# Identity passes ahead of late weights, and a split of the third group's spectra, in a sparse attention plus spectral mixing kernel

## The chip, the cores and the metric

The kernel runs on one core of a Trainium2 chip. The time is the device time of one execution in microseconds (us). Five runs of the kernel before gave a median of 431.25 us (430.57 to 432.88). The profile is of one of these runs, which took 432.25 us.

The engines are TensorE (PE in the profile; PEld is its weight load), VectorE (DVE), ScalarE (ACT), GpSimd (POOL) and SyncE (SP). Transfers run on 16 DMA engines. The weights come in through the queue that POOL issues to, the results go out through SP's.

## The reference

For 8 batches, 8 heads, 576 tokens and a head size of 64, a sparse attention (half of the heads local, half with a stride of 32) gives `x` of 8 x 576 x 512. Then, in the shortest form:

```
X  = rfft(x, axis=1)[:, :64]                 # 64 modes
Yr = Xr @ w_r[m] - Xi @ w_i[m]               # one 512 x 512 pair of weights per mode
Yi = Xr @ w_i[m] + Xi @ w_r[m]
y  = irfft(Y, n=576)
u  = x + y
out = u + relu(u @ w_ch)                     # float32, 8 x 576 x 512
```

The weights `w_r` and `w_i` are 64 x 512 x 512 float32 each, 134 MB in all, and each is used once.

## The kernel before, in words

**The modes.** A mode has two halves (256 rows of the weights each), so there are 128 half-modes, walked in the list `ORDER`. `w_fetch` (line 155) fetches two neighbouring modes of a half into one tile `wt` with 128 partitions: the real part goes to partitions 0 to 63, the imaginary part to 64 to 127, and the transfer turns float32 into float16. Normally that is one transfer of 512 KB for the real and one for the imaginary part. For the last two tiles (modes 60 and 61, modes 62 and 63 of the second list) each mode has a transfer of its own, 256 KB each, in the order: real of the first mode, real of the second, imaginary of the first, imaginary of the second (line 180). Tiles live in a pool of five buffers; after every second mode `mode` (line 544) calls `w_fetch`, whose transfer waits until TensorE has done with the buffer that it takes. POOL's queue is in order, and each of its transfers also waits for the one eight before it.

`mode(slot, m)` makes 16 matmuls (128 x 16, line 555) into a PSUM tile `y`; every eight modes the tile is moved to `Y0` or added into `YT` (lines 581 and 583). The last two modes, 62 and 63, have a small addition of their own.

**The last stage.** The last 24 half-modes are in the list `rest` (line 978), counted by `i` from 0. Between them stand the pieces of the list `late` (line 896), handed out by a share of their number (line 983): from `i` = 1 on, `i` + 1 pieces have been done after mode number `i`, and none after `i` = 0. The pieces are, in this order:

- `spec_pair(2, bq)` for the two halves of the batch (line 874). Spectra of group 2 (modes 32 to 47, already complete) are multiplied with `w_ch` into `zp` (4 matmuls, line 672) and turned into `yp` (4 matmuls, line 679). Both lie in one PSUM pair tile `u`. Then for each of four batches `spec_out` (line 685) copies 32 rows of `zp` to `zzs[b]` with ScalarE (line 687, in the profile line 241) and 32 rows of `yp` to `yys[b]` with VectorE (line 688). The scheduling layer orders two engines' reads of one PSUM tile one behind the other, as they are written.
- `renew(b, ts)` (line 881), 20 times: the kept product `v0` is put into a PSUM tile `v` by an identity matmul (line 889), the group's rows are added (line 696), ScalarE copies it back to `v0` (line 891, shown as 241); then the same rows for `u`, which VectorE adds to `xo` (line 894). It takes two token blocks at a time; four times (after the odd batches) it takes one, the last 64 tokens of two batches. `v` has one buffer, `u` has two.

After mode 61 (`i` = 21) `v_early(0)` and `u_early(0)` put the first output item's kept values into PSUM by identity matmuls (lines 921 and 930), and between modes 62 and 63 `u_early(1)` does so for the second.

**The tail.** When mode 63 is in, the spectra of the last group are made (lines 996 and 997), and for 20 output items in turn the last rows are added (line 941), ScalarE takes the relu (line 955), VectorE adds (line 963) and SyncE writes to memory (lines 971 and 974).

Of the kernel before, what the change touches and what calls it, by code (L numbers as in the profile page):

```python
# [15 lines left out]
B = 8  # L16
# [40 lines left out]
def kernel(  # L57
# [10 lines left out]
    nc = tc.nc  # L68
# [16 lines left out]
    def psum(kind, half=False, pair=False):  # L85
        if pair:
            return pss[kind].tile([128, 2, 512], FP, tag=kind, name=kind)
        if half:
            return pss[kind].tile([128, 1024], F16, tag=kind, name=kind)
        return pss[kind].tile([128, 512], FP, tag=kind, name=kind)  # L90
# [19 lines left out]
    idn = cs["cI"]  # L110
# [44 lines left out]
    def w_fetch(n=1):  # L155
        for _ in range(n):
            i = len(w_tiles)
            if i >= 2 * NM:
                return
            half, m = ORDER[i]  # L160
            if i // 2 in GUEST:
                wt = big.tile([128, 2, 4, DM], F16, tag=GUEST[i // 2], name="wt")
            else:
                wt = pw.tile([128, 2, 4, DM], F16, tag="w", name="wt")
            for ri, src in enumerate((moe_w_r, moe_w_i)):
                dst = wt[ds(64 * ri, 64)]
                rows = src[m : m + 2, ds(256 * half, 256), :].rearrange(
                    "m (p c) e -> p m (c e)", c=4
                )
                dst = dst.rearrange("p m c e -> p m (c e)")  # L170


                ones = range(2)
                if ri and not m:
                    ones = [1]
                elif i < 2 * NM - 4:
                    nc.gpsimd.dma_start(dst, rows)  # L177
                    continue
                for j in ones:
                    nc.gpsimd.dma_start(dst[:, j], rows[:, j])  # L180
            w_tiles.extend((wt[:, 0], wt[:, 1]))

    def w_ch_fetch():
# [56 lines left out]
    def act_copy(out, in_):  # L240
        nc.scalar.activation(out=out, in_=in_, func=ACTF.Copy)  # L241
# [302 lines left out]
    def mode(slot, m):  # L544
        half = 1 - slot
        mi, mg = m % 8, m // 8
        if mi == 0:
            ypt[slot] = psum("y")
        yp = ypt[slot]
        yv = yp.rearrange("p (m e x) -> p m e x", m=8, e=4)  # L550
        wt = w_tiles[ORDER.index((half, m))]
        pr = ds(0, 128 if m else 64)
        for e in range(4):
            for c in range(4):
                nc.tensor.matmul(  # L555
                    yv[:, mi, e, :],
                    wt[pr, XC[c], ds(128 * e, 128)],
                    Xh[half][pr, c, :, :, m],
                    start=(c == 0),
                    stop=(c == 3),  # L560
                )
        if m % 2 and (slot or m // 2 not in GUEST):
            w_fetch()
        ends = {7: 8}
        if slot and mg == 7:
            ends = {5: 6, 7: 2}
        if mi in ends:
            n = ends[mi]
            m0 = mi + 1 - n
            part = (  # L570
                slice(None),
                slice(None),
                mg // 2,
                slice(None),
                ds(8 * (mg % 2) + m0, n),
            )
            src = yp.rearrange("p (m e x) -> p e x m", m=8, e=4)[:, :, :, ds(m0, n)]
            if slot == 0:
                if m == 7:
                    spectra_tile("Y0")  # L580
                nc.scalar.activation(out=YS["Y0"][part], in_=src, func=ACTF.Copy)
            else:
                nc.vector.tensor_tensor(
                    out=YS["YT"][part], in0=src, in1=YS["Y0"][part], op=AluOp.add
                )
# [51 lines left out]
    v0s, xos = {}, {}  # L637
# [31 lines left out]
    def spec_z(g, bq, zp):  # L669
        for e in range(4):  # L670
            lhs = YS["YT"][:, e, g, ds(8 * bq, 8), :].rearrange("p x m -> p (x m)")
            nc.tensor.matmul(
                zp, lhs, w_chs["n"][:, e, :], start=(e == 0), stop=(e == 3)
            )

    def spec_y(g, bq, yp):
        for e in range(4):
            lhs = YS["YT"][:, e, g, ds(8 * bq, 8), :].rearrange("p x m -> p (x m)")
            nc.tensor.matmul(yp[:, ds(128 * e, 128)], lhs, idn, start=True, stop=True)

    def spec_mm(g, bq, yp, zp):
        spec_z(g, bq, zp)
        spec_y(g, bq, yp)

    def spec_out(g, b, yp, zp):
        src, dst = ds(32 * (b % 4), 32), ds(32 * g, 32)
        act_copy(zzs[b][dst], zp[src])
        nc.vector.tensor_copy(out=yys[b][dst], in_=yp[src])

    def rows_of(b, t, acc, spectra, fresh):  # L690
        if t < 4:
            todo = [(acc, out_cols(t), b)]
        else:
            todo = [(acc[ds(64 * j, 64)], ds(512, 64), b - 1 + j) for j in range(2)]
        for o, cols, bb in todo:
            nc.tensor.matmul(  # L696
                o, cA[0:96, cols], spectra[bb][0:96], start=fresh, stop=True
            )
# [75 lines left out]
    for b in range(B):  # L774
# [12 lines left out]
        n = 0  # L787
        nm = NMODES[b]
        for mi in range(nm):
            upto = -(-len(work) * (mi + 1) // nm)  # L790
            for w in work[n:upto]:
                w()
            n = upto
# [7 lines left out]
    xoh = [ptr.tile([128, DM], F16, name=f"xoh{i}") for i in range(4)]  # L801
    zzs = [ptr.tile([128, DM], F16, name=f"zz{i}") for i in range(B)]
    yys = [ptr.tile([128, DM], F16, name=f"yy{i}") for i in range(B)]
# [56 lines left out]
    n = 0  # L860
    for m in range(SPLIT0):
        mode(1, m)
        upto = -(-len(work) * (m + 1) // SPLIT0)
        for w in work[n:upto]:
            w()
        n = upto
# [4 lines left out]
    yctx = ctx.enter_context(ExitStack())  # L871
    pss["y"] = yctx.enter_context(tc.tile_pool(name="ps_y2", bufs=2, space=PSUM))

    def spec_pair(g, bq):
        up = psum("u", pair=True)
        zp, yp = up[:, 0], up[:, 1]
        spec_mm(g, bq, yp, zp)
        for b in range(4 * bq, 4 * bq + 4):
            spec_out(g, b, yp, zp)

    def renew(b, ts):
        n = len(ts)
        if n == 2:
            v0, xo = v0s[b][:, ts[0] : ts[0] + 2], xos[b][:, ts[0] : ts[0] + 2]
        else:
            v0, xo = v0h[b // 2].unsqueeze(1), xoh[b // 2].unsqueeze(1)
        vp, up = psum("v", pair=True), psum("u", pair=True)
        for j, t in enumerate(ts):
            nc.tensor.matmul(vp[:, j], idn, v0[:, j], start=True, stop=False)
            rows_of(b, t, vp[:, j], zzs, False)  # L890
        act_copy(v0, vp[:, 0:n])
        for j, t in enumerate(ts):
            rows_of(b, t, up[:, j], yys, True)
        nc.vector.tensor_tensor(out=xo, in0=up[:, 0:n], in1=xo, op=AluOp.add)  # L894

    late = [lambda bq=bq: spec_pair(2, bq) for bq in range(2)]
    for b in range(B):
        for t in (0, 2):
            late.append(lambda b=b, t=t: renew(b, (t, t + 1)))
# [3 lines left out]
    def units_of(item):  # L903
        P, t = item
        return [(2 * P + j, t) for j in range(2 if t < 4 else 1)]

    items = []
# [5 lines left out]
    vps, ups, rls, osbs = {}, {}, {}, {}  # L913

    def own(item, kept, half):
        P, t = item
        return [kept[b][:, t] for b, _ in units_of(item)] if t < 4 else [half[P]]
# [5 lines left out]
    def v_early(k, stop=False):  # L923
        vps[k] = psum(("v", "v2")[k % 2], pair=True)
        v_own(k, stop)

    def u_early(k):
        ups[k] = psum("u", pair=True)
        for j, r in enumerate(own(items[k], xos, xoh)):
            nc.tensor.matmul(ups[k][:, j], idn, r, start=True, stop=False)  # L930

    def new_rows(k, acc, spectra):
        P, t = items[k]
# [45 lines left out]
    n = 0  # L979
    NL = len(rest) - 2  # L980
    for i, (slot, m) in enumerate(rest):
        mode(slot, m)
        upto = min(len(late), -(-len(late) * i // (NL - 1)))
        for w in late[n:upto]:
            w()
        n = upto
        if i == NL - 1:
            v_early(0)
            u_early(0)
        elif i == NL:  # L990
            u_early(1)
    yctx.close()
    with tc.tile_pool(name="ps_s", bufs=1, space=PSUM) as pss["s"]:
        zp = pss["s"].tile([128, 512], FP, name="zp")
        yp = pss["s"].tile([128, 512], FP, name="yp")
# [15 lines left out]
    for k in range(2, LAST + 2):  # L1011
        if k <= LAST:
            v_early(k)
        if k == 4:
            held = vps[k][:, 1]
            spec_z(3, 1, held)
        if k == 5:
            held = vps[k][:, 1]
            spec_y(3, 1, held)
        if k > 2:  # L1020
            u_early(k - 1)
        if k <= LAST:
            new_rows(k, vps[k], zzs)
        if k > 2:
            new_rows(k - 1, ups[k - 1], yys)
        if k <= LAST:
            v_done(k)
        if k in (4, 5):
            act_copy((zzs, yys)[k - 4][1], held)
        if k > 2:  # L1030
            u_done(k - 1)
# [31 lines left out]
```

The softmax here doesn't subtract the row's maximum and nothing guards it: scores larger than these inputs give would overflow.

## Time and profile before

| what | value |
|---|---|
| median of 5 runs | 431.25 us |
| the profiled execution: time, span | 432.25 us, 430.5 us |
| busy: PE, DVE, ACT, POOL | 347.9, 238.9, 205.7, 107.4 us |
| moved by DMA | 91.78 MB, of which 81.28 MB on POOL's queue |
| weights: transfers of 512 KB | 62 and 60, 18 to 19 us from issue to landing |

The span is the time between the first and the last instruction. The part of the execution outside it is 1.75 us. "Busy" of TensorE is not TensorE at its peak: its matmuls overlap. The row PEclk tells the share of its full clock that TensorE was granted. The DMA row and its GB/s tell how full the 16 transfer engines were.

### The profile page before, as it was taken

The numbers are of one execution on the slowest core, as the hardware profiler recorded it, in microseconds if no ns is written. First come the engines' busy times: TensorE is split into PE (matmuls) and PEld (weight loads), VectorE is DVE, ScalarE is ACT, GpSimd is POOL, SyncE is SP. The second block draws the span as 40 slices with busy tenths as digits, with TensorE's granted clock in tenths as the row PEclk, the third lists the DMA queues.
The fourth block names the chain that finished last, engine by engine and source line by source line (L and its number), as shares of the span: only waits on it lengthen the run. The fifth ranks groups of instructions, "written<-read, shape, count | busy, mean of one in ns | idle before, by whom it ended". The sixth has DMA issues, their size and how long they took to land.

```text
span 430.5 us, 12303 instructions
## 1 busy us (share of the span) xinstructions
PE 347.9 (81%) x5431; PEld 240.9 (56%) x5431; DVE 238.9 (55%) x465; ACT 205.7 (48%) x361; POOL 107.4 (25%) x191
## 2 busy tenths in 40 slices
PE   2977888779989787987477698888898759987994
PEld 2866776658767575765345455565565525543331
DVE  3788778835425444443104246854784455554784
ACT  1687678644645454656132223522442354443773
POOL 8332332322423222221221222222222212310000
PEclk9999899966969998899756769988999968999997
DMA  8999999999999999999999999999999999992698
GB/s 150 209 211 213 212 214 212 211 210 212 214 212 214 214 213 214 214 214 211 212 213 214 213 214 214 215 212 213 213 214 215 213 214 214 213 208 51 238 359 282
DMA packets 30485, 91.78 MB, mean 213 GB/s; under 512 B 4001, under 2 KB 4769, under 8 KB 30433
## 3 DMA queue, kind: packets, MB, share of 16 engines
q0 software_dynamic: 24704, 81.28, 95.5%
q1 hardware_dynamic: 5216, 9.52, 6.2%
q8 instruction: 42, 0.69, 0.6%
q10 hardware_dynamic: 512, 0.21, 0.2%
q14 instruction: 11, 0.08, 0.0%
HBM read 162.83 MB, written 9.44 MB: 400 GB/s over the span
## 4 chain that ended last, share of the span: by engine, by line
DMA 51%; PE 27%; DVE 11%; ACT 5%; issue 3%; POOL 1%; DVEq 0%; ACTq 0%; POOLq 0%
DMA wt<-in_moe_w_i_dram 43%; DMA wt<-in_moe_w_r_dram 7%; PE y L555 4%; DVE xb L231 3%; DVE kz L273 3%; PE v L921 2%; PE tp L403 2%; PE y L522 2%; PE u L930 2%; PE sc L449 2%; PE sc L522 2%; ACT X L241 2%; PE v L941 1%; PE sc L465 1%; DMA ring<-in_v_dram 1%
## 5 line engine op out<-in xcount | busy, mean ns | idle before, releaser
L555 PE MATMUL y<-X,wt 128*128 128x16 f16 (+1 forms) x2048 | 82.7, 192 | 29.8 <-DMA wt<-in_moe_w_i_dram 28.5
L555 PEld LDWEIGHTS <-wt 128*128 128x128 f16 (+1 forms) x2048 | 72.7, 101 | 43.9 <-issue 35.9
L177 POOL DMA_DIRECT2D wt<-in_moe_w_r_dram x62 | 36.4, 588 | 168.3 <-PE y L555 97.9
L177 POOL DMA_DIRECT2D wt<-in_moe_w_i_dram x60 | 35.4, 591 | 49.6 <-DMA wt<-in_moe_w_i_dram 38.1
L653 PE MATMUL sc<-w_cp,xT 128*128 128x512 f16 (+1 forms) x160 | 46.7, 419 | 0.0
L662 ACT ACTIVATE v<-sc 128x512 f16<-128x512 f32 x32 | 19.1, 597 | 55.9 <-PE sc L653 55.8
L479 ACT ACTIVATE PL<-sc 128x480 f16<-128x480 f32 (+1 forms) x48 | 27.3, 579 | 34.4 <-PE sc L465 34.1
L663 DVE COPY xo<-tp 128x512 f16<-128x512 f16 x32 | 22.1, 691 | 32.2 <-PE tp L661 32.1
L231 DVE TENSOR_TENSOR xb<-av,rec 90x256 f16<-90x256 f32 (+2 forms) x80 | 36.0, 450 | 2.7
L230 DVE RECIPROCAL rec<-av 90x4 f32<-90x4 f32 (+2 forms) x80 | 14.6, 183 | 35.9 <-PE av L494 24.5
L410 DVE COPY qT<-tp 128x576 f16<-128x576 f16 x16 | 12.0, 758 | 35.5 <-PE tp L403 32.6
L894 DVE TENSOR_TENSOR xo<-u,xo 128x1024 f16<-128x1024 f32 x16 | 19.6, 1225 | 15.9 <-PE u L696 15.8
L241 ACT ACTIVATE v<-tp 128x640 f16<-128x640 f16 (+1 forms) x24 | 19.4, 808 | 17.7 <-PE tp L437 15.1
L403 PE MATMUL tp<-cI_s,ring 64*64 64x64 f16 x864 | 25.5, 205 | 2.5 <-issue 1.6
L368 ACT ACTIVATE PL<-sc 90x360 f16<-90x360 f32 (+1 forms) x48 | 22.7, 490 | 7.0 <-PE sc L361 6.4
L963 DVE TENSOR_TENSOR osb<-u,rl 128x1024 f32<-128x1024 f32 (+1 forms) x21 | 22.2, 1071 | 5.5 <-PE u L941 3.4
L241 ACT ACTIVATE v<-v 128x1024 f16<-128x1024 f32 x16 | 16.4, 1023 | 18.0 <-PE v L696 18.0
L403 PEld LDWEIGHTS <-ring 64*64 64x64 f16 x864 | 19.7, 118 | 7.7 <-issue 3.9
L449 PE MATMUL sc<-cMl_s,cI_s 128*128 128x480 f16 (+1 forms) x48 | 20.7, 430 | 3.3 <-ACT PL L479 1.6
L266 PE MATMUL tp<-cI_s,ring 72*128 72x72 f16 x256 | 15.4, 207 | 8.8 <-DMA ring<-in_v_dram 7.2
L955 ACT ACTIVATE rl<-v 128x1024 f32<-128x1024 f32 (+1 forms) x21 | 18.8, 901 | 6.6 <-PE u L941 4.1
L522 PEld LDWEIGHTS <-xb 108*128 108x128 f16 (+2 forms) x176 | 15.2, 106 | 12.0 <-DVE xb L231 7.4
(128 smaller groups left out, 695.8 us busy)
## 6 DMA issues: line engine op xcount, KB each, us to landing
wt<-in_moe_w_r_dram POOLq DMA_DIRECT2D x62, 512.0 KB, 18.2
wt<-in_moe_w_i_dram POOLq DMA_DIRECT2D x60, 512.0 KB, 19.4
out_dram<-osb SPq DMA_DIRECT2D x15, 512.0 KB, 3.2
ring<-in_v_dram POOLq DMA_DIRECT2D x8, 288.0 KB, 13.4
ring<-in_q_dram POOLq DMA_DIRECT2D x8, 288.0 KB, 13.5
ring<-in_k_dram POOLq DMA_DIRECT2D x8, 288.0 KB, 13.0
ring<-in_v_dram POOLq DMA_DIRECT2D x3, 512.0 KB, 14.5
ring<-in_q_dram POOLq DMA_DIRECT2D x3, 512.0 KB, 14.7
```

Source lines behind the costliest of these rows:

```text
L177: nc.gpsimd.dma_start(dst, rows)
L231: nc.vector.tensor_tensor(out=dst, in0=val.rearrange("p h (q c) -> p h c q", c=4), in1=rec[0:n, 0:pieces] .to_broadcast((n, pieces, 64)) . ...
L241: nc.scalar.activation(out=out, in_=in_, func=ACTF.Copy)
L368: nc.scalar.activation(out=PS[0:n, ds(POFF[t], 4 * n)], in_=scp[0:n, 0 : 4 * n], func=ACTF.Exp, scale=SCALE,)
L403: nc.tensor.transpose(tp[ds(64 * hp, 64), ds(64 * i, 64)], qn[ds(64 * hp, 64), ds(64 * (9 * g + i), 64)], idn[ds(64 * hp, 64), ds(64 * hp, ...
L449: nc.tensor.matmul(scp[:, 0 : n * times].rearrange("p (h x) -> p h x", h=times), idn, mask_rows("cMl", n, times), start=True, stop=False,)
L479: nc.scalar.activation(out=dst, in_=src, func=ACTF.Exp, scale=SCALE)
L522: nc.tensor.matmul(xp[:, ds(192 * cp, 192)].rearrange("p (f m) -> p f m", f=3), xb[b][0:n, base + t, ds(128 * cp, 128)], F[0:n, :, t, :], ...
L555: nc.tensor.matmul(yv[:, mi, e, :], wt[pr, XC[c], ds(128 * e, 128)], Xh[half][pr, c, :, :, m], start=(c == 0), stop=(c == 3),)
L653: nc.tensor.matmul(vp[pr, :], xT[:, ch, cols], w_chs["cp"][:, ch, :], start=(ch == 0), stop=(ch == 3),)
L663: nc.vector.tensor_copy(out=xo[pr].rearrange("p (h q c) -> p h q c", h=2, c=4), in_=tp[pr, 0:512].rearrange("p (h c q) -> p h q c", h=2, c=4),
L963: nc.vector.tensor_tensor(out=osb[:, j], in0=up[:, j], in1=rl[:, j], op=AluOp.add)
```

## The change

1. The third group's spectra (group 2) are split: `spec_late` does the `z` part for both halves of the batch in one `u` tile, and later the `y` part in another; ScalarE reads the first alone, VectorE the second alone. The `z` part now stands after the first of the 24 modes, the `y` part after the second; `late` still has 22 pieces, and after mode number `i` exactly `i` + 1 of them are done.
2. `fill` makes identity matmuls whose result is overwritten: five after the `y` part, into a `v` tile that nobody reads, and three ahead of each of the four `renew` of one block, into the tile that the next matmul starts afresh.
3. `u_early(1)` between modes 62 and 63 makes its two identity matmuls three times over; only the last time counts.
4. The 256 KB parts of the last two weight tiles are issued mode by mode: real and imaginary part of the first mode, then those of the second.

```diff
@@ w_fetch
+            single = []
             for ri, src in enumerate((moe_w_r, moe_w_i)):
...
-                for j in ones:
-                    nc.gpsimd.dma_start(dst[:, j], rows[:, j])
+                single += [(j, ri, dst[:, j], rows[:, j]) for j in ones]
+            for _, _, to, rows in sorted(single, key=lambda x: x[:2]):
+                nc.gpsimd.dma_start(to, rows)
@@ last stage
-    def spec_pair(g, bq):
+    def spec_late(mm, kept, eng):
         up = psum("u", pair=True)
-        zp, yp = up[:, 0], up[:, 1]
-        spec_mm(g, bq, yp, zp)
-        for b in range(4 * bq, 4 * bq + 4):
-            spec_out(g, b, yp, zp)
+        for bq in range(2):
+            mm(2, bq, up[:, bq])
+        for b in range(B):
+            eng(kept[b][64:96], up[ds(32 * (b % 4), 32), b // 4])
+
+    def fill(acc, n):
+        for _ in range(n):
+            nc.tensor.matmul(acc, idn, v0s[0][:, 0], start=True, stop=True)
@@ renew
         vp, up = psum("v", pair=True), psum("u", pair=True)
+        if n == 1:
+            fill(vp[:, 0], 3)
@@
-    late = [lambda bq=bq: spec_pair(2, bq) for bq in range(2)]
+    def spec_last():
+        spec_late(spec_y, yys, lambda o, i: nc.vector.tensor_copy(out=o, in_=i))
+        fill(psum("v", pair=True)[:, 0], 5)
+
+    late = [lambda: spec_late(spec_z, zzs, act_copy), spec_last]
@@ u_early
-    def u_early(k):
+    def u_early(k, times=1):
         ups[k] = psum("u", pair=True)
-        for j, r in enumerate(own(items[k], xos, xoh)):
-            nc.tensor.matmul(ups[k][:, j], idn, r, start=True, stop=False)
+        rows = list(enumerate(own(items[k], xos, xoh)))
+        for n, (j, r) in enumerate(rows * times):
+            nc.tensor.matmul(
+                ups[k][:, j], idn, r, start=True, stop=n < len(rows) * (times - 1)
+            )
@@ the walk over rest
-        upto = min(len(late), -(-len(late) * i // (NL - 1)))
+        upto = min(len(late), i + 1)
...
-            u_early(1)
+            u_early(1, times=3)
```

## The prediction

> **What bounds the kernel now.** I read the page first, then the chain that ended last, then busy times by stretch, then the timeline of two places: 340 to 360 us and 383 to 396 us.
>
> ```profile
> PE 347.9 (81%) x5431; PEld 240.9 (56%) x5431; DVE 238.9 (55%) x465; ACT 205.7 (48%) x361; POOL 107.4 (25%) x191
> ...
> PEclk9999899966969998899756769988999968999997
> DMA  8999999999999999999999999999999999992698
> ...
> DMA 51%; PE 27%; DVE 11%; ACT 5%; issue 3%; POOL 1%; DVEq 0%; ACTq 0%; POOLq 0%
> ```
>
> The transfer engines are full from the second slice to slice 36, about 387 us, and half of the chain is weights landing. Until the last weight is in, TensorE's speed counts only where TensorE is late for a weight; after it, TensorE sets the end. The chain, in order of time, shows the hand-over:
>
> ```profile
> 383.64 10.74 DMA wt<-in_moe_w_i_dram
> 394.38 0.14 issue
> 394.51 0.65 PE y L555 x16
> 395.16 0.02 issue
> 395.19 0.30 DVE YT L583
> ```
>
> So 394.38 is the last landing, and whatever delays mode 63's matmuls (394.51) delays all that follows. Behind it the chain is TensorE without gaps until 424 us (items of some 1.3 us). By stretch (PE busy, PEld, DVE, ACT, POOL, granted clock, DMA share, GB/s):
>
> ```profile
> 343.64:347.06 3.42, 1.59 (x21) 0.88 (x22) 2.08 (x4) 1.76 (x3) 0.59 (x1) 1.00 1.06 213
> 347.06:357.30 10.24, 6.65 (x46) 3.00 (x47) 5.09 (x6) 4.13 (x6) 1.18 (x2) 0.50 1.07 214
> ...
> 391.43:394.84 3.41, 2.42 (x33) 1.25 (x33) 0.63 (x2) 0.32 (x1) 0.00 (x0) 1.00 0.17 34
> ```
>
> The clock fell to half for 10.24 us after a stretch with 46% of busy time; the transfers stayed full beside it. In the stretch ahead of the tail TensorE was 71% busy and the clock stayed whole. The two places in the timeline:
>
> ```profile
> 341.60 0.58 ACT L241 ACTIVATE zz<-u 32x512 f16<-32x512 f32 x1 [2.33 <-PE u L679]
> ...
> 342.21 0.68 DVE L688 CAST yy<-u 32x512 f16<-32x512 f32 x1 [2.62 <-ACT zz L241]
> 342.93 0.59 ACT L241 ACTIVATE zz<-u 32x512 f16<-32x512 f32 x1 [0.75 <-DVE yy L688]
> ...
> 352.04 0.59 PE L889 MATMUL v<-v,cI_s 128*128 128x512 f16 x1 [3.59 <-ACT v L241]
> ```
>
> ```profile
> 383.49 0.64 PE L555 MATMUL y<-X,wt 128*128 128x16 f16 x16 [0.50 <-DMA wt<-in_moe_w_i_dram]
> ...
> 391.80 0.59 PE L921 MATMUL v<-v,cI_s 128*128 128x512 f16 x2 [0.47 <-ACT v0h L241]
> ...
> 392.23 0.59 PE L930 MATMUL u<-xo,cI_s 128*128 128x512 f16 x2
> ...
> 393.28 0.64 PE L555 MATMUL y<-X,wt 128*128 128x16 f16 x16 [0.46 <-DMA wt<-in_moe_w_i_dram]
> ...
> 393.76 0.59 PE L930 MATMUL u<-xo,cI_s 128*128 128x512 f16 x2
> ...
> 394.51 0.64 PE L555 MATMUL y<-X,wt 128*128 128x16 f16 x16 [0.16 <-DMA wt<-in_moe_w_i_dram]
> ```
>
> The first shows ScalarE and VectorE taking turns, each released by the other, and TensorE waiting 3.59 us for them. The second shows mode 58 (383.49), which waited for its weight: by then TensorE had caught up what it lost at 342 to 358. Then come the last modes, with small waits ahead of 62 and 63.
>
> **z and y apart: 0 us.** Sixteen copies in turn, 8 x 0.59 + 8 x 0.69 plus hand-overs of 0.02 to 0.04, run from 341.60 to 351.66. Afterwards ScalarE's eight take 4.8 us side by side with VectorE's 5.6, from about 341.7 and 343.0. The first `renew` then needs its `u` buffer from the z copies (346.5), the second from the last y copy (348.6). Mode 60 of the first list runs at 349.1 (weights in at 348.99) in place of 354.55: TensorE is some 5 us earlier there. None of it reaches the end: from mode 58 on, at 383.36, TensorE waits for weights in both kernels. What hides it is the weight stream; without that cover up to 5 us would show. What is late next is the next tile, one every 4.9 us. The z matmuls (1.72 us, two chain pieces of 0.86) now stand ahead of mode 57, so the POOL transfer that waits for the end of that mode (issued 342.13) goes some 0.3 us later. Behind it in POOL's queue stand only further weights, seven transfers are still under way, and a transfer lands 18 us after its issue: 0 us. Nothing is moved past SP's queue.
>
> **The passes behind the y part, and three `renew`: 0 us.** A 128x512 pass steps by 0.215 us (0.43 for two, 392.23 to 392.66). Five make 1.08 us, from 343.0 to 344.1, in a wait that ends with the landing at 344.04. Three make 0.65 in each `renew` of one block. That `renew` with its mode takes about 1.4 us (380.13 to 381.5), 2.1 with the passes, and a weight comes every 2.45. If the cover were gone, these would cost 1.08 + 3 x 0.65 = 3.0 us; the 0.53 us of slack ahead of mode 58 says that it is there.
>
> **The last `renew`, +0.65; u_early, +0.86; their cover, -0.94.** Mode 61 starts at 389.71, held by a landing at 389.57 (the trace's landing events) that the new order of pieces leaves the fourth of its tile. `renew` begins at 390.40 when ScalarE has freed `v`; three passes put its matmuls, ScalarE's copy (391.15) and `v_early` and `u_early(0)` behind it 0.65 later: `u_early(0)` is through at 393.31, not 392.66. Before, TensorE stood free from 392.66 to 393.28 (0.62) and from 394.19 to 394.51 (0.32). Pieces land 1.2 us apart (390.71, 391.93, 393.14, 394.38). In the new order mode 62 needs the second of them, not the third, so it is ready near 392.05 and waits for TensorE: 393.31. Its sixteen matmuls step to 393.79 (0.48), the six passes to 395.08 (6 x 0.215). The last piece lands at 394.38 as before, so mode 63 starts at 395.08, not 394.51. VectorE's addition behind the `renew` (391.37) slides to 392.7 at the latest, before `u_early(1)` needs its buffer. On the path: 0.65 + 0.86 - 0.94 = **+0.57 us**.
>
> **The clock: 0 in the sum, -1.7 to 0 as bounds.** The clock records come in steps of 3.41 us. Over such stretches at full clock, it fell after those with up to 69% of PE busy time (39.86 us) and stayed after some with 66% (323.16 us). Slid along the end, the stretches that begin between 389.8 and 394.6 us have 68 to 76%: the edge of it, and where the steps fall differs between executions. If it falls there, one step at half clock in the tail costs 3.41 / 2 = 1.7 us, and the passes would save that; they fill up to 1.5 of the 3.41 us. In this profile the clock was 1.00 from 357.30 to the tail's end, so I take 0. A loss has no row for it: the passes only add busy time.
>
> [...]
>
> **Sum.** Against the profiled execution: 432.25 + 0.57 = 432.8 us (span 431.1 and the same 1.75 around it). That run lay 1.0 above the median, and everything else in it is common, so the median goes to 431.25 + 0.57 = **431.8 us**. What a measurement of this kernel can tell from no change is about 0.3%, 1.3 us: 429.96 to 432.54 counts as the same.
>
> **Rivals.**
> 1. *The passes have no cover (slower).* Place: between modes 61 and 63. Price: all of 0.65 + 0.86 = 1.51 us, 432.8. It needs the last two tiles in memory before TensorE asks, that is, the 0.94 us of waits gone; it counts as slower from a cover below 0.2. For it: all pieces of one tile come within 4.9 us, and TensorE's rate there (2.1 us for a mode with its `renew`) hardly beats the weights' 2.45. Against: three waits of TensorE for weights in these 12 us (383.49, 393.28, 394.51). Chance 0.20.
> 2. *Hidden anyway.* If the last piece lands 0.6 us later against mode 61's, the passes end in time: 431.25. For it: landings vary. Against: the steps of 1.2 us are even. Chance 0.12.
> 3. *The clock does fall in most executions before (faster).* For it: the 68 to 71% above, at the edge. Against: it did not fall in the profiled run, which is slower than three of the other four. One step saved: 431.25 - 1.7 + 0.57 = 430.1, still the same; two steps: 428.4. Chance 0.15, of which 0.10 beyond the bound.
> 4. *The new order evens the end of the stream (faster).* From 387 to 392 us half of the transfer capacity is in use (DMA shares near 0.5). If real and imaginary parts side by side filled both halves, the stream would end near 391.5, 3 us sooner: 428.8. Against: each piece lands in steps on all 16 engines, the same ones late for every piece. Chance 0.05.
>
> **How the numbers follow.** My forecast, +0.57, has 0.48; its own range is 431.2 to 432.5, from the landings' play. The same within 0.3%: 0.48 + 0.12 + 0.05 = 0.65. Slower: 0.20, the first rival. Faster: 0.10 + 0.05 = 0.15. The range goes from one clock step saved (430.1) to the uncovered passes and 0.4 more for a median of few runs, 433.2.
>
> **What the next profile would show.** Right: ScalarE's eight zz copies back to back, then VectorE's eight; clock whole through 340 to 360; TensorE waiting for weights at every second mode from 349 on; no weight wait at modes 62 and 63, and mode 63 about 5.4 us after mode 61 where it was 4.8. Wrong: a weight wait still ahead of mode 63 (rival 2); modes 60 to 62 without any weight wait (rival 1); DMA shares above 0.5 after 387 us (rival 4). A lower clock in the tail, or a last landing that moves by more than 1 us against the start, would break the sum.

## The result, and the profile after

The changed kernel takes **432.42 us**, the median of 42 executions (431.71 to 433.62). The kernel before has 431.47 us over 71 executions (430.48 to 435.81; the 431.25 ahead of the prediction was the median of the first five). The ratio is 1.0018, 95% interval 1.0009 to 1.0027: +0.78 us on 431.5, between +0.39 and +1.16. That is a little slower, and inside the 0.3% that counts as the same. The profiled execution took 433.29 us with a span of 431.4.

The page of the changed kernel, the lines that answer to those shown of before:

```profile
PE 353.1 (82%) x5452; PEld 243.1 (56%) x5452; DVE 239.0 (55%) x465; ACT 205.7 (48%) x361; POOL 107.4 (25%) x191
...
PEclk9999999858997878896856669998999989899998
DMA  8999999999999999999999999999999999992697
...
q8 instruction: 43, 0.70, 0.6%
```

TensorE has 21 matmuls more (5452 against 5431) and as many weight loads, so 42 instructions. The transfer engines are full for as long as before. The last line was not shown of before: q8 is a queue of packets of 16 KB each that the profile calls "instruction", and before it held 42 of them. In the trace of before one of these packets comes for every 255 TensorE instructions or so (238 have started at the first packet, 10685 at the last), so they are read here as fetches of TensorE's code. One packet more looks like nothing; the experiments say otherwise.

The chain of what ended last in the changed kernel, around the last modes (start us, us, what):

```profile
393.11 0.43 PE u L943 x2
393.55 0.47 PE y L557 x16
394.02 1.29 PE u L943 x6
395.31 0.49 PE y L557 x16
395.80 0.02 issue
395.82 0.30 DVE YT L585
```

Before, the piece ahead of mode 63 was a weight landing. Now it is six passes of `u_early(1)`, 1.29 us of TensorE. The trace's landing events put the last piece at 394.46 us, and mode 63 starts at 395.15: 0.69 us later, where before it was 0.13. **The difference, 0.56 us, is the predicted +0.57.** How far this profile stands for others is a question that the experiments answer below.

The timeline of the changed kernel, first at the two late copies, then at the last modes (start us, us, engine, line, operation; in brackets the idle time before it and what ended it):

```profile
341.84 4.79 ACT L243 ACTIVATE zz<-u 32x512 f16<-32x512 f32 x8 [2.50 <-PE u L674]
342.46 1.24 PE L885 MATMUL v<-v,cI_s 128*128 128x512 f16 x5
342.72 5.61 DVE L905 CAST yy<-u 32x512 f16<-32x512 f32 x8 [3.05 <-PE u L681]
...
390.47 0.81 PE L885 MATMUL v<-v,cI_s 128*128 128x512 f16 x3 [0.19 <-ACT v L243]
391.87 0.60 ACT L243 ACTIVATE v0h<-v 128x512 f16<-128x512 f32 x1 [1.45 <-PE v L698]
392.52 0.59 PE L933 MATMUL v<-v,cI_s 128*128 128x512 f16 x2 [0.47 <-ACT v0h L243]
392.95 0.59 PE L943 MATMUL u<-xo,cI_s 128*128 128x512 f16 x2
393.38 0.64 PE L557 MATMUL y<-X,wt 128*128 128x16 f16 x16
393.86 1.46 PE L943 MATMUL u<-xo,cI_s 128*128 128x512 f16 x6
395.15 0.64 PE L557 MATMUL y<-X,wt 128*128 128x16 f16 x16
```

The copies, in turn for 10 us before, run side by side in 4.79 and 5.61 us. Modes 62 and 63 no longer wait for a weight: neither of the `L557` lines has a bracket.

Busy time by stretch of the changed kernel (PE busy, PEld, DVE, ACT, POOL, granted clock, DMA share, GB/s):

```profile
343.40:346.80 3.40, 1.94 (x23) 1.00 (x22) 3.31 (x5) 3.32 (x7) 0.59 (x1) 1.00 1.07 216
346.80:350.30 3.50, 3.50 (x24) 1.53 (x23) 2.73 (x4) 1.40 (x2) 1.18 (x2) 0.51 1.04 210
350.30:360.00 9.70, 8.89 (x110) 4.99 (x109) 5.59 (x5) 4.76 (x6) 2.36 (x4) 1.00 1.07 214
```

The fall of the clock here lasts one step, 346.84 to 350.25, in place of the 10.24 us of before (a second one, at 374.15, lasts one step too). Over all profiles of this document, the seven with the split have none to two steps at half clock between 340 and 361 us, the seven without it three or four. The fall still came, after a stretch with 57% of busy time in which TensorE's longest wait was 0.92 us, although the prediction had it gone. The transfers stayed full beside it.

So the path is as forecast and the median is some 0.2 to 0.4 us above it. Two questions stand: is the +0.57 what makes the kernel slower (and not the clock, the order of the pieces or the split), and is there another term?

### The profile page after: what moved, and what is told of

Read it like the earlier page. It is cut to its first block, busy times and chain, and to the rows that moved or that the text cites. A ratio compares the mean times of both kernels' runs of the same rounds, so it can differ in the third digit from the quotient of the medians.

```text
span 431.4 us, 12346 instructions
## 1 busy us (share of the span) xinstructions
PE 353.1 (82%) x5452; PEld 243.1 (56%) x5452; DVE 239.0 (55%) x465; ACT 205.7 (48%) x361; POOL 107.4 (25%) x191
## 5 line engine op out<-in xcount | busy, mean ns | idle before, releaser
L557 PE MATMUL y<-X,wt 128*128 128x16 f16 (+1 forms) x2048 | 82.9, 192 | 30.8 <-DMA wt<-in_moe_w_i_dram 29.4
L557 PEld LDWEIGHTS <-wt 128*128 128x128 f16 (+1 forms) x2048 | 73.0, 102 | 45.4 <-issue 38.0
```

What stands on the lines that cost most here:

```text
L557: nc.tensor.matmul(yv[:, mi, e, :], wt[pr, XC[c], ds(128 * e, 128)], Xh[half][pr, c, :, :, m], start=(c == 0), stop=(c == 3),)
```

## The experiments

Three theories. **Path**: the passes in the last modes hold TensorE beyond the last landing, as the prediction's sum has it. **Clock**: the passes keep the clock up, so that part of their cost comes back. **Code fetch**, formed after the first two groups: with the added instructions one more block of TensorE code is fetched before the end, among the writes of the results. The kernels ran in three groups; the kernel before had medians of 431.29, 431.40 and 431.44 us beside them (35 executions each), and each kernel below had 10 to 12. The table measures every kernel by three numbers of its profile: how long mode 63 starts after the last landing, when TensorE code was last fetched before the last issue, and the time from the last result's issue to the end.

| Kernel | mode 63 after last landing, us | last fetch of code at, us | last issue to end, us | median, us | against before in its group, us | ratio, 95% |
|---|---|---|---|---|---|---|
| before, profiled for the prediction | 0.13 | 401.8 | 5.21 | | | |
| before, run as an experiment (G) | 0.13 | 401.3 | 4.69 | 431.63 | +0.19 | 0.9991 to 1.0034 |
| after | 0.69 | 420.3 | 5.54 | 432.42 | +0.95 | 1.0009 to 1.0027 |
| A1 no passes in the last `renew` | 0.14 | 421.5 | 4.95 | 432.26 | +0.97 | 0.9989 to 1.0031 |
| A2 `u_early(1)` once | 0.13 | 420.5 | 5.07 | 431.85 | +0.56 | 0.9988 to 1.0026 |
| A3 `u_early(1)` five times | 1.79 | 420.7 | 5.30 | 433.38 | +1.98 | 1.0023 to 1.0069 |
| B before, with `u_early(1)` three times | 0.72 | 422.4 | 6.20 | 432.82 | +1.53 | 1.0009 to 1.0048 |
| C no passes at all | 0.14 | 401.7 | 4.66 | 431.53 | +0.24 | 0.9968 to 1.0027 |
| D old order of the pieces | 0.87 | 419.5 | 5.39 | 432.48 | +1.08 | 1.0000 to 1.0043 |
| E1 before, early work taken out | 0.13 | 404.5 | 4.61 | 434.01 | +2.61 | 1.0030 to 1.0072 |
| E2 E1 with passes in its place | 0.13 | 422.6 | 5.57 | 433.04 | +1.64 | 1.0012 to 1.0054 |
| F1 after, with 32 matmuls fewer | 1.26 | 402.4 | 5.36 | 432.09 | +0.65 | 1.0005 to 1.0025 |
| F2 before, with 32 matmuls fewer | 1.32 | 408.6 | 5.11 | 431.71 | +0.27 | 0.9996 to 1.0029 |
| H before, with 8 matmuls more, early | 0.14 | 421.4 | 5.68 | 432.11 | +0.67 | 0.9992 to 1.0030 |

For after, the difference is against the 71 executions above. G is the same program as before, so its +0.19 shows what a median of 12 executions can be off by.

### A1, A2, A3: one part of the passes more or less

A1, of the changed kernel:

```diff
-        if n == 1:
+        if n == 1 and b < B - 1:
             fill(vp[:, 0], 3)
```

> The changed kernel without the three passes of the last one-block renew (the other fills, the tripled u_early, the split and the new order of pieces stay). Theory 1 (only the passes between modes 61 and 63 reach the end, less the 0.94 us of waits there): mode 62 starts at 392.7, when TensorE is through with u_early(0) and no longer at 393.3; six passes end at 394.5, where the last landing lets mode 63 start anyway: 0.0 us against the kernel before (ratio 1.000). Rival (0.2 to 0.4 us of the measured 0.8 to 0.9 come from the new order of pieces or the split): +0.3 us, ratio 1.0007.

A2, and A3 with `times=5`:

```diff
-            u_early(1, times=3)
+            u_early(1)
```

> The changed kernel with u_early(1) made once, not three times over. Theory 1: mode 62 at 393.3, u_early(1) through at 394.2, mode 63 waits for the landing at 394.4 as before: 0.0 us against the kernel before (ratio 1.000). Rival (the rest of the change costs 0.2 to 0.4 us): +0.3 us, ratio 1.0007.

> The changed kernel with u_early(1) made five times over, four passes more. Theory 1: there is no cover left, so each pass costs its whole 0.215 us: +0.86 us on the changed kernel, which is +1.4 to 1.8 us on the kernel before (ratio 1.0033 to 1.0041). Rival (the passes lie in a wait): less than +0.4 us on the changed kernel, ratio below 1.003.

Measured: 432.26 (A1), 431.85 (A2) and 433.38 us (A3). In the profiles of A1 and A2 mode 63 starts 0.14 and 0.13 us after the last landing: either half alone, 0.65 or 0.86 us, fits under the cover of 0.94, as the sum said. In A3 nothing hides any more. TensorE's lines in the timeline of A3:

```profile
392.93 0.64 PE L557 MATMUL y<-X,wt 128*128 128x16 f16 x16
393.40 2.32 PE L943 MATMUL u<-xo,cI_s 128*128 128x512 f16 x10
395.56 0.59 PE L557 MATMUL y<-X,wt 128*128 128x16 f16 x16
```

Ten passes stand between mode 62 and mode 63, 2.16 us from start to start where after had 1.29: +0.87 for four, against the predicted 0.86. The median is 0.96 above that of after, and its +1.98 lies a little above the +1.4 to +1.8 that was expected. What follows: beyond the landing a pass costs its 0.215 us in full, and the rival that it would be hidden anyway is refuted. But A1 and A2, whose passes are hidden, have medians 0.97 and 0.56 above before, where the path says 0. That was a miss; their intervals (each about 0.9 us to either side) hold both answers, so it pointed to a second term and did not prove one.

### B: the tripled `u_early(1)` alone, in the kernel before

```diff
-    def u_early(k):
+    def u_early(k, times=1):
         ups[k] = psum("u", pair=True)
-        for j, r in enumerate(own(items[k], xos, xoh)):
-            nc.tensor.matmul(ups[k][:, j], idn, r, start=True, stop=False)
+        rows = list(enumerate(own(items[k], xos, xoh)))
+        for n, (j, r) in enumerate(rows * times):
+            nc.tensor.matmul(
+                ups[k][:, j], idn, r, start=True, stop=n < len(rows) * (times - 1)
+            )
...
-            u_early(1)
+            u_early(1, times=3)
```

> The kernel before with nothing but the tripled u_early(1) between modes 62 and 63. Theory 1: mode 62 is held to 393.3 by its weights, four more passes cost 0.86 us of which the wait of 0.32 us ahead of mode 63 takes a part: +0.54 us against the kernel before (ratio 1.0013), almost the whole of the change. Rival (passes cost less and the rest comes from elsewhere): +0.2 us or less, ratio 1.0005.

TensorE's lines in the timeline of B:

```profile
392.99 0.64 PE L555 MATMUL y<-X,wt 128*128 128x16 f16 x16
393.47 1.46 PE L931 MATMUL u<-xo,cI_s 128*128 128x512 f16 x6
394.76 0.64 PE L555 MATMUL y<-X,wt 128*128 128x16 f16 x16
```

The last landing was at 394.04, so mode 63 starts 0.59 us later than the 0.13 of before; the path's own price was 0.86 - 0.32 = 0.54. The median rose by 1.53, though, and the ratio's interval begins at +0.39 us. The place to look is behind the last issue: 6.20 us to the end, the longest of all. The page of B has 43 packets on q8 with only eight instructions more than before.

### C: the split and the order alone

Of the changed kernel, all passes are taken out; the z and y copies stay apart and the pieces keep the new order.

```diff
-        if n == 1:
-            fill(vp[:, 0], 3)
...
-        fill(psum("v", pair=True)[:, 0], 5)
...
-            u_early(1, times=3)
+            u_early(1)
```

> The changed kernel without any of the added passes: only the split of z and y and the new order of pieces stay. Theory 1: mode 62 starts at 392.7 and mode 63 waits for the last landing at 394.4: 0.0 us (ratio 1.000) against the kernel before; TensorE is some 5 us earlier at 350 us and waits for weights from there on. Rival (split or order move the stream's end): +0.3 us, ratio 1.0007, with the last landing later against the start of the stream.

Measured: 431.53 us, +0.24, which is what G, the unchanged kernel, shows against itself. Mode 63 starts 0.14 after the landing and q8 has 42 packets. The split of z and y brings mode 60 of the first list to 350.39 us, 4.2 us earlier than before, and is worth nothing that this can tell in the median.

### D: the old order of the pieces

```diff
-            for _, _, to, rows in sorted(single, key=lambda x: x[:2]):
+            for _, _, to, rows in single:
                 nc.gpsimd.dma_start(to, rows)
```

> The changed kernel with the pieces of the last two tiles in the old order. Theory 1: mode 62 needs the third piece, which lands near 393.2, just ahead of 393.3 when TensorE gets there: the same as the changed kernel, +0.6 to 0.9 us on the kernel before (ratio 1.0014 to 1.002). Rival (the new order moves the last landing): 0.3 us less than the changed kernel, ratio 1.001 or below.

Measured: 432.48 us, +1.08, as good as after's +0.95. In D's profile the third piece lands at 392.27 and mode 62, which needs it, starts at 392.65, when TensorE is through with `u_early(0)`: it no longer waits for the piece, because the passes make TensorE later than that anyway. The order of the pieces costs and brings nothing that these medians can tell. The rival that it evens the end of the stream falls too: in the profile of after the DMA share from 388 to 392 us is 0.54, as before.

### E1, E2: a tail with a fallen clock, and the same tail with passes

E1 takes the early matmuls out of the waits before modes 62 and 63 of the kernel before and does them behind mode 63, so that TensorE idles there. E2 fills the same waits with six overwritten passes.

```diff
-        if i == NL - 1:
+        if i == NL + 1:
             v_early(0)
             u_early(0)
-        elif i == NL:
             u_early(1)
```

> The kernel before with v_early(0), u_early(0) and u_early(1) moved behind mode 63, so that between modes 61 and 63 TensorE has only the last renew and mode 62. Both theories count six passes (1.29 us) behind mode 63, of which some 0.5 us lie in the wait for VectorE's addition: +0.75 us. Clock by the share of busy time (theory 2): every 3.41 us stretch laid over 389 to 395 us then holds one of 20 to 62% busy time, below the 69% at which the clock fell, so the clock falls to half in the tail in nearly every execution, for one or two steps: 1.7 to 4 us more, 434 to 436 us in all, like the four executions of the kernel before at 435.3 to 435.8. [...]

```diff
         if i == NL - 1:
-            v_early(0)
-            u_early(0)
+            vps[0] = psum("v", pair=True)
+            for _ in range(4):
+                nc.tensor.matmul(vps[0][:, 0], idn, v0s[0][:, 0], start=True, stop=True)
         elif i == NL:
+            for _ in range(2):
+                nc.tensor.matmul(vps[0][:, 0], idn, v0s[0][:, 0], start=True, stop=True)
+        elif i == NL + 1:
+            v_own(0)
+            u_early(0)
             u_early(1)
```

> The same as the run with the emptied stretch (the six early passes behind mode 63), but six identity passes that are overwritten stand where the early ones stood: same work behind mode 63, same busy stretch as in the kernel before. Theory 2: the clock stays whole or falls as seldom as before, +0.75 us, 432.2 us, 1.7 to 4 us below the emptied one. Rival: no difference from the emptied one.

Busy time by stretch of E1 (columns as above):

```profile
390.01:393.42 3.41, 1.41 (x22) 0.57 (x19) 1.89 (x3) 0.77 (x2) 0.00 (x0) 1.00 0.35 70
393.42:400.24 6.82, 5.91 (x43) 2.70 (x40) 0.82 (x2) 0.60 (x1) 0.00 (x0) 0.50 0.00 1
```

and of E2:

```profile
390.95:394.37 3.42, 2.46 (x28) 1.04 (x24) 1.07 (x2) 0.60 (x1) 0.00 (x0) 1.00 0.25 49
394.37:397.78 3.41, 2.99 (x30) 1.73 (x31) 0.67 (x2) 0.56 (x1) 0.00 (x0) 1.00 0.00 0
```

The stretches are laid where the clock records lie: E1's clock falls at 393.42. With TensorE 41% busy (1.41 of 3.41) in the step up to there, the clock goes to a half for the next 6.8 us; in E2 the step ahead of mode 63 is 72% busy, and the clock stays whole. Mode 63 starts at 394.34 in both. From VectorE's addition behind it to the last issue E1 takes 33.11 us and E2 30.80: the two steps at half clock cost **2.31 us**. The end differs by less, 1.35, because E2 has a code fetch at 422.6 and takes 5.57 us from the last issue to the end where E1 takes 4.61. The medians differ by 0.97 (434.01 and 433.04): E1 came out at the low end of what theory 2 had, and E2 0.8 us above its 432.2; the fetch, which was not counted, is the likely reason. So in this pair the passes did hold the clock up (1.00 where E1 has 0.50), and the fallen clock cost 2.31 us of the tail. But the kernel before, with 71% in that stretch, has a whole clock there and 30.07 us from that addition to the last issue; so have after, G, C, H, F1, F2, A1, A2, A3, B and D (30.06 to 30.08). In none of these profiles is there anything for the passes to save.

### F1, F2: is it the fetch of code?

By now every profile with a pass or two more had a fetch of TensorE code near 421 us, and none without had one. F1 is the changed kernel with so many matmuls left out earlier that this fetch does not come before the end: in four modes of the first list, two of four chunks are left out, 32 matmuls in all. F2 leaves out the same in the kernel before. (These modes run at 110 to 120 us; the expectations name another list and place.)

```diff
+        left_out = slot == 0 and m in (9, 11, 13, 15)
         for e in range(4):
-            for c in range(4):
+            for c in (0, 3) if left_out else range(4):
```

> The changed kernel with 64 instructions of TensorE fewer: four early modes (9, 11, 13 and 15 of the second list, near 200 us, while the weight stream sets the pace) leave out the middle two of their four channel blocks, so their spectra are not the reference's. TensorE's program is then 22 instructions shorter than in the kernel before instead of 42 longer. Theory 3 (the added instructions bring a 43rd fetch of 16 KB of TensorE's code, near 420 us, while the results' writes fill all 16 transfer engines, which costs 0.5 to 1 us at the end): 42 fetches, none between 405 and 428 us, last issue to end 4.7 us instead of 5.0 to 6.2, and only the 0.57 us of the passes remain: 431.9 us, ratio 1.0013. Rival (the fetch is hidden, the excess is the passes' or the split's): as the changed kernel, 432.4 us, ratio 1.0022.

> The kernel before with the same 64 early instructions left out (the same four modes' middle channel blocks, so the same spectra are not the reference's), as the control for leaving them out. Theory 3: nothing on the path changes, 431.3 us, ratio 1.000; a code fetch that now falls at the program's very end is gone, so the part of the time outside the span stays at 1.8 us in every run (in some runs of the kernel before it is 2.4 to 3.6). Rival (leaving early matmuls out speeds the kernel by itself): below 430.9 us, ratio 0.999 or less.

Measured: F1 432.09 us (+0.65, ratio 1.0015 [1.0005, 1.0025]), F2 431.71 (+0.27). F1's page has 42 packets on q8, its last fetch lies at 402.4, and its median is 0.33 below after's: about what the path alone asks. Mode 63 follows mode 61 by 5.52 us, as in after (5.51), so the passes are on the path as before; but here the last landing came earlier against mode 61, and mode 63 is late by 1.26 us where after had 0.69. One expectation missed: F1's last issue to the end took 5.36 us and not some 4.7, so this time also plays by some tenths without a late fetch.

Another expectation came true, and it tells where the fetch was before. In F2 the part of the time outside the span is 1.7 to 1.8 us in every execution, and it is at most 1.9 in every kernel with a fetch near 421; in the kernel before it reaches 3.6, and it goes over 3 in E1 and G. The trace of E1, which has as many TensorE instructions as before, has a 43rd packet on q8 at 433.59 us, 0.85 behind its span's end. So the added instructions do not so much add a block of code as move its fetch from behind the end into the writes of the results.

F2's median, +0.27, is near G's +0.19. Its profile has something else, in these stretches (columns as above):

```profile
347.90:351.40 3.50, 1.08 (x18) 0.76 (x19) 2.06 (x3) 1.86 (x4) 0.91 (x2) 1.00 1.08 217
351.40:358.30 6.90, 4.13 (x25) 1.76 (x25) 3.83 (x4) 2.96 (x4) 0.27 (x1) 0.51 1.05 212
```

The clock fell here for two steps in the middle of the stall, after one step at 341.2 already. This time TensorE did not catch up: mode 58 started at 384.64, 0.78 us after its weight had landed (383.86), and mode 63 at 395.08, 1.3 us after the last landing. H, below, is the other such profile: its mode 58 starts at 383.44, 0.54 us after its landing at 382.90, but there TensorE had caught up by mode 63. So the cover that the prediction gives the split (mode 58 waits for its weight) is there in twelve profiles and not in these two. Both lack the split, and no run shows what it would have saved in them.

Leaving matmuls out moves every later fetch of code, too, and one of them lies among the last weights. A 256 KB piece lands in 16 parts (so many landing events has each in the trace of before). In before the last part came 0.3 us behind the last but one until the fetch at 387.40, and 1.5 us behind it in the first piece that landed afterwards (389.58); it stayed some 1.4 us behind up to the last landing. The same jump, to 0.9 to 1.5 us, stands in thirteen of the fourteen profiles at the first piece that lands after the fetch at 386 to 389 us, in F1 and H one or two pieces later, as their fetch is. F2 alone, whose fetch comes at 392.53, has 0.4 us throughout. So a fetch probably also holds up the last landings, from which the cover between modes 61 and 63 is made, and F1 and F2 change more than the fetch at the end.

### G, H: the fetch by itself

H adds eight matmuls to the kernel before, at a place far ahead of the end: two overwritten passes in each of four calls of `spec`.

```diff
     def spec(g, bq):
         yp, zp = psum("tp"), psum("av")
+        for _ in range(2):
+            nc.tensor.matmul(zp, idn, w_chs["n"][:, 0, :], start=True, stop=True)
         spec_mm(g, bq, yp, zp)
```

> The kernel before with eight overwritten identity passes (16 instructions) in the four earlier calls of spec, near 260 to 315 us, where TensorE waits for weights. Theory 3: mode 63 starts as in the kernel before, as soon as the last weight is in, and the tail's TensorE part is the same 30.1 us, but a 43rd code fetch stands near 422 us and last issue to end is 0.5 to 1 us longer: 432.0 us, ratio 1.0012 to 1.0023. Rival (code fetches are hidden): 431.3 us, ratio 1.000.

G is the kernel before, unchanged:

> The kernel before, unchanged, run as if it were another. All theories: ratio 1.000; its twelve runs show how far medians of twelve play (0.2 us expected from the spread of the others), and its profile is a second one of the kernel before: no code fetch between 405 and 428 us, last issue to end near 4.7 us, mode 63 within 0.15 us of the last landing. Rival to theory 3 (the excess is play of the runs): its median lies 0.5 us or more from the kernel before's.

The two profiles agree to 0.01 us from the last landing (393.90) to the issue of the last result: mode 63 at 394.04 (H) and 394.03 (G), 394.71 for the addition behind it and 424.78 for the last issue in both. (Ahead of that they differ: mode 61 starts at 389.87 in H and at 389.42 in G.) Then H ends at 430.46 and G at 429.47. The DMA view of G from 405 to 431 us (queue, engine and count of the issues, KB each, median us to landing):

```profile
out_dram<-osb SPq DMA_DIRECT2D x12, 512.0 KB, 3.1
...
out_dram<-osb ACTq DMA_DIRECT2D x1, 128.0 KB, 3.6
```

and of H:

```profile
q8 instruction: 1, 0.02, 0.3%
...
out_dram<-osb SPq DMA_DIRECT2D x12, 512.0 KB, 3.4
...
out_dram<-osb ACTq DMA_DIRECT2D x1, 128.0 KB, 4.3
```

One packet of 16 KB on q8, at 421.4 us, on one of the 16 engines for 1.26 us; the writes beside it land later, the last ones by 0.7 us. By stretch, G and then H (columns as above):

```profile
426.00:428.00 2.00, 0.00 (x0) 0.00 (x0) 0.00 (x0) 0.00 (x0) 0.00 (x0) 0.57 0.86 277
428.00:430.00 2.00, 0.00 (x0) 0.00 (x0) 0.00 (x0) 0.00 (x0) 0.00 (x0) 0.50 0.00 0
```

```profile
426.00:428.00 2.00, 0.00 (x0) 0.00 (x0) 0.00 (x0) 0.00 (x0) 0.00 (x0) 0.50 0.94 277
428.00:430.00 2.00, 0.00 (x0) 0.00 (x0) 0.00 (x0) 0.00 (x0) 0.00 (x0) 0.50 0.05 14
```

All engines of both have finished, and G's writes are through by 428 while H's reach beyond it. The medians are 432.11 (H) and 431.63 (G): +0.48, or +0.67 against before in the group.

The pair alone would not be enough: the first profile of the kernel before, also without a fetch there, has 5.21 us from the last issue to the end, 0.52 more than G. The landings of the single writes decide it. The write that is issued 4.57 us ahead of the last one lands after 4.57 us in H and after 3.02 in G. Over all profiles it takes 3.01 to 3.32 us in the six without a fetch near 421 and 3.86 to 5.36 in the eight with one; no value of the one set reaches the other. In B, E2 and H, whose fetch comes latest against the last issue, the write issued 1.3 us earlier still lands after 2.9 us, as in G.

How much of this is the fetch? Over all profiles in the table, the time from the last issue to the end has a mean of 5.46 us in the eight with a fetch near 421 (4.95 to 6.20) and of 4.94 in the six without (4.61 to 5.36): **0.52 us**, with the two sets overlapping: the last writes make up a part of what the earlier ones lost, and in before, F1 and F2 they land some tenths late without a fetch, for a reason that no run shows. That can be tested on the medians, which did not enter it. Add to 0.52 the path by the prediction's prices, and for E1 and E2 the tail's own growth over 30.07:

| Kernel | path or tail | fetch | sum | median against before |
|---|---|---|---|---|
| after | 0.57 | 0.52 | 1.09 | +0.95 |
| A1, A2 | 0 | 0.52 | 0.52 | +0.97, +0.56 |
| A3 | 1.43 | 0.52 | 1.95 | +1.98 |
| B | 0.54 | 0.52 | 1.06 | +1.53 |
| C, G, F2 | 0 | 0 | 0 | +0.24, +0.19, +0.27 |
| D | 0.57 | 0.52 | 1.09 | +1.08 |
| E1 | 3.04 | 0 | 3.04 | +2.61 |
| E2 | 0.73 | 0.52 | 1.25 | +1.64 |
| F1 | 0.57 | 0 | 0.57 | +0.65 |
| H | 0 | 0.52 | 0.52 | +0.67 |

All thirteen agree within 0.5 us, which is as much as the term itself. With the path alone, A1, B and E2 would be off by 0.9 to 1.0 and H by 0.7. No single ratio of twelve executions proves the half microsecond, since H's own interval reaches from -0.3 to +1.3 us. Together they do: A1, A2 and H have the fetch and nothing on the path, and their 35 executions have a median of +0.67 against before in their groups; the 36 of C, F2 and G, without either, have +0.20. The two differ by 0.3 to 0.75 us (95%, by resampling).

None of these kernels is faster than the kernel before.

## Why the prediction was right, and where it was not

Point by point, by its own steps:

- **z and y apart, 0 us: right.** C has +0.24 where the unchanged kernel has +0.19. The view that carried it was the wait of mode 58 for its weight. F2 and H showed the limit of that: two profiles without the split in which TensorE came to mode 58 after its weight, in F2 up to mode 63, 1.3 us after the last landing.
- **The passes behind the y part and in three `renew`, 0 us: right on the path.** A1 keeps all of these and tripled `u_early(1)`, and its mode 63 starts at the landing.
- **The last `renew`, +0.65; `u_early`, +0.86; their cover, -0.94: right.** The three prices were predicted from rows of before, and the profile after has 0.81 for three passes with pipeline end (0.65 from start to start), 1.29 for six, and mode 63 late by 0.56 against the landing. Mode 63 came 5.51 us after mode 61, where 5.4 was forecast. A1, A2, B and A3 changed one of the terms each and moved mode 63 in the forecast direction, A3 by 1.66 us where the prices give 1.43. The agreement to 0.01 us is luck all the same: with the whole 1.51 us of passes in place, mode 63 comes 0.56 us later than before's 0.13 in after, 0.74 in D and 1.13 in F1, so the cover was 0.95, 0.77 and 0.38 us in these three profiles.
- **The order of the pieces only makes mode 62 ready earlier: right** (D).
- **The clock in the tail, 0 in the sum: right**, though its bound of -1.7 was a real danger: in E1 the clock fell after a step with 41% of busy time, for two steps and 2.31 us. The stretches slid along the end are 68 to 84% busy, not 68 to 76, which leaves the edge where the prediction saw it. TensorE's longest wait ahead of the fall was 1.94 us in E1, and 1.58 us ahead of the fall at 347.06 us in before.
- **"Clock whole through 340 to 360": wrong, without effect.** It fell for one step at 346.84, mode 60 of the first list ran at 350.32 and not at 349.1, and TensorE's waits at every second mode began at 359.05 and not at 349. The weights hid it.
- **The sum: one term is missing.** The step that fell short is the last one, "everything else in it is common". The 42 added instructions were counted as matmuls of 0.215 us and not as code. They move the fetch of the 43rd block to 420 us, while the results' writes fill all 16 engines (DMA share 1.05 in after during that fetch, from 420.34 to 421.27 us), and that lengthens the time from the last issue to the end by about 0.5 us in the mean (H has 0.99 more than G and 0.47 more than the first profile of before). Path and fetch together, 1.09, lie inside the measured +0.39 to +1.16, and so does the path alone; the forecast of 431.8 was too low by 0.6, of which 0.2 is the better median of before (431.47 for 431.25).

TensorE itself shows no wait for the fetch at 421 us in the pair of G and H: the last issue lies at 424.78 in G, which has none, and in H, which has one. The transfers that the fetch meets do take longer: the write issued 4.57 us ahead of the last one lands after 3.01 to 3.32 us without a fetch and after 3.86 to 5.36 with one.

Of the rivals, the first (no cover) and the second (hidden anyway) are refuted by mode 63's 0.56 us, and the fourth by D and by the DMA share of 0.54. The third, the clock falling in most executions before, is refuted as far as profiles go: G and the profiled run of before both had a whole clock in the tail. What stays open is the seldom case. Above 434 us lie 4 of the 71 executions of before and 4 of the 36 of C, F2 and G; of the 102 of after, A1, A2, B, D and F1, which all have passes between modes 61 and 63, none does, and one of A3's ten (H, without passes there, has none in its 11). So the passes may hold off something that is rare and dear, which a median does not feel. Whether those long ones are a fall of the clock in the tail, or a stall as in F2, no trace of such an execution shows.

## What to carry to other kernels

Price work that is put into a wait by what remains of the wait: two fillings of 0.65 and 0.86 us each fit alone under a cover of 0.94, together they stuck out by 0.57, and every further pass cost its full 0.215 us (A3). Read the cover from more than one profile: here it was 0.4 to 0.95 us. Count added instructions also as code: look at the packets of the instruction queue, and at what the transfer engines carry when a block is fetched. Before filling a wait to save the clock, look whether the clock falls there at all; here it did not, and a busy share of 71% had been enough.

## What the runs showed of the hardware that was not expected

- Eight more TensorE instructions (B) were enough to bring a 16 KB fetch, 1.80 us long on its engine, among writes that fill all 16. The DMA share of after during its fetch, which took 0.93 us, is 1.05. The write issued 4.57 us ahead of the last one, at such a fetch or just behind it, took 3.86 to 5.36 us to land in eight profiles, and 3.01 to 3.32 in the six without it.
- The clock went to half for two steps of 3.41 us after a step with 41% of busy time and no wait over 1.94 us, and stayed whole after steps with 71% (before) and 72% (E2). At the tail those two steps cost 2.31 us, less than the 3.4 that two steps at half speed would lose (2 x 3.41 / 2, an estimate).
- A stall that twelve profiles had made up by mode 58 was not made up in F2 (0.78 us late at mode 58, 1.3 us at mode 63) and in H (0.54 us at mode 58, none at mode 63). Slack read from one profiled execution is not there in each.
